# Separate accumulator banks, two pools for the second layer's banks, and a later split of its first weights

## The chip, the cores and the metric

The kernel runs on one core of a Trainium2 chip. The metric is the device time of one execution in microseconds, and the kernel before takes 818.07 us (median of three runs, 817.4 to 819.8). The core's engines run beside each other, each through its own queue in order: PE (matrix products), ACT (activations and copies), DVE (vector operations), POOL (GpSimd, vector operations too), and SP, which issues the transfers. An instruction waits in its queue until the instructions that produce its inputs, or that last used its buffer, are done.

## What is computed

The reference, cut to what matters:

```python
def _attn_ref(q, k, v, proj):                    # q, k, v: (2, 8, 768, 64), proj: (64, 6)
    q_bits = (np.einsum('bhsd,dk->bhsk', q, proj) > 0)
    k_bits = (np.einsum('bhsd,dk->bhsk', k, proj) > 0)
    mask = bucket(q_bits)[:, :, :, None] == bucket(k_bits)[:, :, None, :]
    scores = np.where(mask, scale * np.matmul(q, k.transpose(0, 1, 3, 2)), -1e9)
    attn = softmax(scores)
    return np.matmul(attn, v)

def _moe_ref(x, w_in, w_out):                    # x: (1536, 512), d_ff 2048
    h = np.maximum(x @ w_in, 0.0)
    return h * h @ w_out

def _moe2_ref(x, w_in, w_out, alpha):            # the same sizes
    h = x @ w_in
    g = np.maximum(h, 0.0) + alpha * np.minimum(h, 0.0)
    return g @ w_out

def reference(...):
    x = _attn_ref(q, k, v, proj) laid out as (1536, 512)
    return _moe2_ref(_moe_ref(x, ...), ...)
```

## The kernel before

The 1536 tokens go in four chunks of 384. Attention of chunk 0 runs alone; then `feed_forward(0)`, `(1)` and `(2)` compute the first layer of one chunk each, and between their steps the attention of the next chunk and the conversion of the weights are issued. `feed_forward(3)` follows with its output transposed (`project_t`), and then the second layer runs in two halves of 768 tokens: `wide_hidden(0)`, `whole_project(0)`, `wide_hidden(1)`, `whole_project(1)`. Every product is made of three matmuls, of operands that are split into a high and a low part: the high part is a rounding copy on ACT, the low part a subtraction on DVE or POOL.

In the first layer a step is one f of 16 (128 columns of d_ff). `hidden(c, f)` makes 12 matmuls (L704 to L706) into a bank, ACT takes the relu `r` out of it (L711) and makes `gh` (L712) and `g` (L714), and a subtraction makes `gl` (L717; on DVE in chunk 3). `project` adds the step before to the accumulators: one PSUM tile `acc` of three banks. After f = 15 of chunks 0 to 2 the banks are copied out in turn by DVE, ACT and DVE (L811, L813), and go to memory as `y`. In chunk 3 `project_t` uses these three banks and a fourth from the pool `ps_s` (L727, L728, and L730 or L735 with `gl`), which DVE and ACT copy out at L802 and L804. The weights of a step are split by ACT (L665, `wh`) and DVE or POOL (L666, `wl`).

In the second layer `wide_hidden(n)` makes, for each f of 8, seven products of 6 matmuls each (L896 to L898), from seven sums of x (`xph`, `xpl`: ACT L855, DVE L856; the plain sums L870, L875, L879 and L883 are DVE's). They are made by `x_sums(n)`. The weights of such an f come as one tile `wraw` (L911), which `w_part` splits: two copies on ACT (L918, 128x1024 and 128x768) and two subtractions on POOL (L919). Sums and the leaky relu (L902, L935, L942, L958) take the products out of the banks. `whole_project(n)` has 16 steps into six accumulator banks (L1000, L1001, L1006; in the last step L1003), which are then copied out by DVE (L1012) and ACT (L1014). Beside `whole_project(0)` go `second_x(2)`, which transposes chunk 2's y back (three blocks of four transposes, L838, each into one bank, copied by ACT at L839), `x_sums(1)`, and at its end the first `w_load` and `w_part` for `wide_hidden(1)`.

Before the change every bank of the second layer comes from one pool `ps2` with eight buffers of one tag, and a request gets a buffer that was given back. The order on each engine is set when the kernel is built, by a scheduler that follows the program, its priorities and its waits for buffers; on the chip each queue keeps that order.

Of the kernel before, what the change touches and what calls it, by code (L numbers as in the profile page):

```python
# [7 lines left out]
F32 = mybir.dt.float32  # L8
# [4 lines left out]
AF = mybir.ActivationFunctionType  # L13
ALU = mybir.AluOpType
PSUM = bass.MemoryType.PSUM
# [14 lines left out]
def kernel(  # L30
# [20 lines left out]
    nc = tc.nc  # L51
# [3 lines left out]
    P = 128  # L55
    T = S // 2
    NTB = T // P
    NKB = S // P
    NPAIR = H // 2
    NCH = NT // T  # L60
    KDM = DM // P
    KFF = w_in1.shape[0]
# [4 lines left out]
    def pool(name, bufs, stack=ctx, **kw):  # L67
        return stack.enter_context(tc.tile_pool(name=name, bufs=bufs, **kw))
# [1 line left out]
    const = pool("const", 1)  # L70
    dram = pool("scr", 1, space=DRAM)
    layer1 = ctx.enter_context(ExitStack())
    ps_s = pool("ps_s", 1, layer1, space=PSUM)
    ps_a = pool("ps_a", 1, layer1, space=PSUM)
    ps_h = pool("ps_h", 1, layer1, space=PSUM)
    ps_m = pool("ps_m", 2, layer1, space=PSUM)
    m1 = pool("m1", 1, layer1, side="right")
    m2 = pool("m2", 2, layer1, side="right")
    state_whole = pool("whole", 4, layer1, side="right")
# [2 lines left out]
    state = {"attention": True, "moe": False, "s": 0, "m": 0, "h": 0, "whole": state_whole}  # L82
# [28 lines left out]
    def h_tile():  # L111

        state["h"] += 1
        if not state["attention"] and state["h"] % 3:
            return ps_m.tile([P, 512], F32, tag="m", name="m")
        return ps_h.tile([P, 512], F32, tag="h", name="h")

    def f32(ap):
        return ap.bitcast(F32)
# [480 lines left out]
    def load_bits(u):  # L600
        l, f, o = u
        t = state["wide"].tile([P, DM, 2], U32, tag="wide", name="wbits")
        nc.sync.dma_start(out=t.rearrange("p n b -> p (n b)"), in_=(WO if o else WI)[l][f].bitcast(U32))
        w_bits[u] = t
# [67 lines left out]
    def units(i):  # L672

        if i >= len(work):
            return []
        return [(0, work[i][1], o) for o in range(2)]

    def fetch(i):

        for u in units(i):  # L680
            w_f[u] = state_whole.tile([P, DM], F32, tag="wf", name="wf")
            if u in w_d:
                nc.sync.dma_start(out=w_f[u], in_=w_d[u])
            else:
                to_f32(u, w_f[u])
                w_d[u] = dram.tile([P, DM], F32, tag="w%d_%d_%d" % u, name="w%d_%d_%d" % u)
                nc.sync.dma_start(out=w_d[u], in_=w_f[u])

    def split(i, o):
        for u in units(i)[o:o + 1]:  # L690
            last = i >= (NCH - 1) * KFF
            split_w(u, nc.gpsimd if (o or i // KFF == 1) and not last else nc.vector)

    def hidden(c, f, x, step):
        xh, xl = x
        wih, wil = w_split.pop((0, f, 0))
        ps = h_tile()
        hp = ps[:, 0:T]
        for kk in range(KDM):
            if kk == KDM // 2:  # L700
                step()
            ks = slice(kk * P, (kk + 1) * P)
            first, last = kk == 0, kk == KDM - 1
            nc.tensor.matmul(hp, wih[:, ks], xh[:, kk, :], start=first, stop=False)  # L704
            nc.tensor.matmul(hp, wih[:, ks], xl[:, kk, :], start=False, stop=False)  # L705
            nc.tensor.matmul(hp, wil[:, ks], xh[:, kk, :], start=False, stop=last)  # L706
        r = m1.tile([P, T], F32, tag="r", name="r")
        g = m1.tile([P, T], F32, tag="g", name="g")
        gh = m2.tile([P, T], F32R, tag="gh", name="gh")
        gl = m2.tile([P, T], F32R, tag="gl", name="gl")  # L710
        nc.scalar.activation(r, hp, AF.Relu)  # L711
        nc.scalar.activation(gh, r, AF.Square)  # L712
        if SQUARE[c] == "a":
            nc.scalar.activation(g, r, AF.Square)  # L714
        else:
            eng[SQUARE[c]].tensor_tensor(g, r, r, ALU.mult)
        (nc.vector if c == NCH - 1 else nc.gpsimd).tensor_tensor(gl, g, f32(gh), ALU.subtract)  # L717
        return gh, gl
# [19 lines left out]
    def project(f, g, acc, step):  # L738
        gh, gl = g
        woh, wol = w_split.pop((0, f, 1))  # L740
        first, last = f == 0, f == KFF - 1
        blocks = [slice(t * P, (t + 1) * P) for t in range(NTB)]

        def high(t):
            nc.tensor.matmul(acc[:, t, :], gh[:, blocks[t]], woh, start=first, stop=False)
            nc.tensor.matmul(acc[:, t, :], gh[:, blocks[t]], wol, start=False, stop=False)

        def low(t):
            nc.tensor.matmul(acc[:, t, :], gl[:, blocks[t]], woh, start=False, stop=last)  # L749

        if last:
            for t in range(NTB):
                high(t)
                low(t)
                step()
        else:
            for t in range(NTB):
                high(t)
                if t < NTB - 1:
                    step()  # L760
            for t in range(NTB):
                low(t)
            step()

    def feed_forward(c, background):

        slots = KFF * 5
        state["slot"] = 0

        turn = c == NCH - 1  # L770

        def step():
            state["slot"] += 1
            background(state["slot"] / slots)

        x = xT.pop(c)
        pend = None
        acc = None
        for f in range(KFF):
            i = index[c, f]  # L780
            split(i + 1, 0)
            split(i, 1)
            g = hidden(c, f, x, step)
            fetch(i + 2)
            for u in units(i + 3):
                if u not in w_d:
                    load_bits(u)
            step()
            if pend is not None:
                if acc is None:  # L790
                    acc = ps_a.tile([P, 3, 512], F32, tag="acc", name="acc")
                    if turn:
                        fourth = ps_s.tile([P, 2, 512], F32, tag="s", name="s")
                        acc = [acc[:, m, 0:T] for m in range(KDM - 1)] + [fourth[:, 0, 0:T]]
                (project_t if turn else project)(*pend, acc, step)
            pend = (f, g)
        (project_t if turn else project)(*pend, acc, step)
        if turn:
            x = new_raw(c)
            for m in range(KDM):  # L800
                if m % 2:
                    nc.vector.tensor_copy(x[:, m, :], acc[m])  # L802
                else:
                    nc.scalar.activation(x[:, m, :], acc[m], AF.Copy)  # L804
            return
        y = m1.tile([P, NTB, DM], F32, tag="y", name="y")
        d = dram.tile([P, NTB, DM], F32, tag=f"y{c}", name=f"y{c}")
        y_d[c] = d
        for t in range(NTB):
            if t % 2 == 0:  # L810
                nc.vector.tensor_copy(y[:, t, :], acc[:, t, :])  # L811
            else:
                nc.scalar.activation(y[:, t, :], acc[:, t, :], AF.Copy)  # L813
        nc.sync.dma_start(out=d, in_=y)


# [4 lines left out]
    def new_raw(c):  # L821
        x_raw[c] = state["xraw"].tile([P, KDM, T], F32, tag="xraw", name="xraw")
        return x_raw[c]
# [64 lines left out]
    def slot(name, dt=F32R):  # L888
        return state["slots"].tile([P, 2048], dt, tag="slot", name=name)

    def bank():
        return state["ps"].tile([P, 512], F32, tag="b", name="b")

    def products(ps, w, m, gh, gl, first, last):
        ms = slice(m * P, (m + 1) * P)
# [9 lines left out]
    raw_sums = {}  # L905
    loaded = {}

    def w_load(f):
        if f < NF:
            raw_sums[f] = slot("wraw", F32)[:, 0:7 * HM].rearrange("p (a n) -> p a n", n=HM)  # L910
            nc.sync.dma_start(out=raw_sums[f], in_=w_sum[f])  # L911

    def w_part(f):
        if f < NF:
            w = raw_sums.pop(f)
            t = [slot("wp")[:, 0:7 * HM].rearrange("p (a n) -> p a n", n=HM) for _ in range(2)]
            for i, j in ((0, 4), (4, 7)):
                nc.scalar.activation(t[0][:, i:j], w[:, i:j], AF.Copy)  # L918
                nc.gpsimd.tensor_tensor(t[1][:, i:j], w[:, i:j], f32(t[0][:, i:j]), ALU.subtract)  # L919
            loaded[f] = t  # L920

# [104 lines left out]
    for i in range(2):  # L1026
        low_ins, sm_ins = scored[0, 2, 2 * NTB - 1] if i == 0 else scored[0, 3, NTB - 1]
        with tc.issue_after(low_ins.ins), tc.issue_after(sm_ins.ins):
            fetch(i)
            if i == 0:  # L1030
                split(0, 0)
    state["moe"] = True


    steps, ends = attention_beside()
# [15 lines left out]
    for c in range(NCH - 1):  # L1051
        feed_forward(c, lambda x: beside(c + x))
# [17 lines left out]
        reason="needed late only",  # L1070
# [4 lines left out]
    feed_forward(NCH - 1, turned)  # L1075
    w_load(0)
    w_load(1)
    w_part(0)
    layer1.close()
    state["ps"] = pool("ps2", 8, space=PSUM)  # L1080
    state["g"] = pool("g", 1, side="right")
    state["sums"] = pool("sums", 2, side="right")
    state["out"] = pool("out", 2, side="right")

    steps = second_x(2, bank) + x_sums(1)

    def beside_project(f):
# [76 lines left out]
```

## Time and profile before

| | us |
|---|---|
| median of three runs | 818.07 |
| the three runs | 819.8, 818.07, 817.4 |
| the profiled execution | 819.41 |
| its span, first to last instruction | 817.4 |
| PE busy in the span | 776.8 |
| DVE busy | 545.8 |
| ACT busy | 505.8 |
| POOL busy | 313.3 |

The profiled execution has 2.0 us around its span. By stage, chunk 3 of the first layer lies from 490 to 560 us of the span, `wide_hidden(0)` from 560 to 622, `whole_project(0)` to 683 or so, `wide_hidden(1)` to 750, and the last projection behind it. A row of a timeline gives the start, the duration, the engine, the line and operation with its output and inputs, how many instructions the row holds, and, in brackets, how long the engine had been idle and what ended that.

### The profile page before, as it was taken

To read this page: it belongs to the slowest core of one execution; us is meant where nothing else is said; L and a number is where in the kernel's file an instruction comes from. 1 tells how busy PE (TensorE), PEld (TensorE's weight loads), DVE (VectorE), ACT (ScalarE), POOL (GpSimd) and SP (SyncE) were. 2 spreads that over 40 slices of the span, in tenths; PEclk is the share of its full clock that TensorE was granted. 3 is DMA by queue.
4 is the path that set the end of the run, shared out by engine and by line. 5 is a ranking of instruction groups with operands and counts; after the bars stand their busy time and mean duration, and the time that the engine had idled before them with its cause. 6 is when DMAs were issued, how large, how long until landed. Compare 5 with 4: busy or idle time off the path is not lost.

```text
span 817.4 us, 12516 instructions
## 1 busy us (share of the span) xinstructions
PE 776.8 (95%) x4330; PEld 634.9 (78%) x4330; DVE 545.8 (67%) x876; ACT 505.8 (62%) x988; POOL 313.3 (38%) x231
## 2 busy tenths in 40 slices
PE   6999899999999999999999998999999999999998
PEld 3665777776768767677776878999998888999886
DVE  8678899887757667788977956754665732665111
ACT  5778778766656556565665648764765525776331
POOL 1012323232356645643342355001563446663440
PEclk9999999999999999999999999999999999999999
DMA  6857878778678787677677568530311226421222
GB/s 181 212 159 229 259 228 269 241 218 243 174 223 265 225 226 242 210 242 264 203 237 232 174 218 286 171 130 1 135 27 52 65 95 221 141 68 44 65 65 90
DMA packets 56707, 143.66 MB, mean 176 GB/s; under 512 B 7402, under 2 KB 11652, under 8 KB 56644
## 3 DMA queue, kind: packets, MB, share of 16 engines
q1 hardware_dynamic: 56644, 142.87, 55.6%
q8 instruction: 34, 0.56, 0.3%
q14 instruction: 29, 0.24, 0.1%
HBM read 96.62 MB, written 25.47 MB: 149 GB/s over the span
## 4 chain that ended last, share of the span: by engine, by line
PE 44%; DVE 4%; DMA 3%; ACT 3%; issue 2%; POOL 1%; SPq 0%; ACTq 0%; POOLq 0%; DVEq 0%
PE b L1000 5%; PE b L1001 5%; PE b L1006 5%; PE b L896 4%; PE b L898 4%; PE b L897 4%; PE m L425 2%; PE h L704 1%; PE s L386 1%; PE h L705 1%; PE h L706 1%; PE acc L749 1%; PE m L409 1%; PE acc L728 1%; PE acc L735 1%
## 5 line engine op out<-in xcount | busy, mean ns | idle before, releaser
L666 POOL TENSOR_TENSOR wl<-wf,wh 128x512 fp32r<-128x512 f32 x64 | 89.0, 1393 | 82.1 <-ACT wh L665 76.4
L665 ACT ACTIVATE wh<-wf 128x512 fp32r<-128x512 f32 x128 | 79.5, 628 | 49.4 <-PE h L705 24.0
L919 POOL TENSOR_TENSOR wp<-wraw,wp 128x1024 fp32r<-128x1024 f32 (+1 forms) x32 | 68.4, 2161 | 99.8 <-ACT wp L918 92.1
L394 ACT ACTIVATE sm<-s,low 128x768 f32<-128x768 f32 x84 | 75.6, 901 | 45.9 <-DVE low L391 45.6
L717 POOL TENSOR_TENSOR gl<-g,gh 128x384 fp32r<-128x384 f32 x48 | 53.1, 1106 | 131.4 <-ACT g L714 64.9
L391 DVE TENSOR_REDUCE low<-s 128x1 f32<-128x768 f32 x84 | 80.0, 953 | 32.9 <-PE s L386 32.4
L990 POOL TENSOR_TENSOR gp<-g,gp 128x768 fp32r<-128x768 f32 x32 | 60.6, 1894 | 81.6 <-ACT gp L989 81.4
L386 PE MATMUL s<-k,q 128*128 128x384 f32 x336 | 80.0, 357 | 10.8 <-ACT sm L394 9.7
L409 PE MATMUL m<-ident,sm 128*128 128x128 f32 x531 | 85.4, 277 | 4.9 <-DVE pt L415 2.4
L409 PEld LDWEIGHTS m<-ident,sm 128*128 128x128 f32 x531 | 65.4, 141 | 22.7 <-DVE pt L415 3.4
L704 PE MATMUL h<-xh,wh 128*128 128x384 f32 x212 | 77.9, 367 | 2.1 <-DVE u L472 1.7
L386 PEld LDWEIGHTS s<-k,q 128*128 128x128 f32 x336 | 58.1, 192 | 26.9 <-ACT sm L394 16.8
L896 PE MATMUL b<-xph,wp 128*128 128x384 f32 x224 | 75.3, 343 | 3.4 <-DVE b L942 1.9
L1000 PE MATMUL b<-wp,gp 128*128 128x512 f32 x192 | 75.1, 391 | 0.0
L898 PE MATMUL b<-xph,wp 128*128 128x384 f32 x224 | 75.0, 335 | 0.0
L897 PE MATMUL b<-xpl,wp 128*128 128x384 f32 x224 | 75.0, 335 | 0.0
L1001 PE MATMUL b<-wp,gp 128*128 128x512 f32 x192 | 74.8, 389 | 0.0
L706 PE MATMUL h<-xh,wl 128*128 128x384 f32 x212 | 72.3, 341 | 0.3 <-POOL wl L666 0.3
L705 PE MATMUL h<-xl,wh 128*128 128x384 f32 x212 | 72.3, 341 | 0.0
L986 DVE TENSOR_TENSOR wp<-wp 128x512 fp32r<-128x512 f32 x28 | 23.1, 830 | 67.6 <-ACT wp L985 67.5
L425 PE MATMUL m<-pt,vr 128*64 128x384 f32 x336 | 66.2, 498 | 0.6 <-ACT pt L413 0.6
L666 DVE TENSOR_TENSOR wl<-wf,wh 128x512 fp32r<-128x512 f32 x64 | 50.9, 804 | 21.3 <-ACT wh L665 20.8
(180 smaller groups left out, 1829.8 us busy)
## 6 DMA issues: line engine op xcount, KB each, us to landing
wf<-w SPq DMA_DIRECT2D x96, 256.0 KB, 3.2
wbits<-in_w_in_dram SPq DMA_DIRECT2D x32, 512.0 KB, 4.6
wbits<-in_w_out_dram SPq DMA_DIRECT2D x32, 512.0 KB, 4.2
wraw<-ws SPq DMA_DIRECT2D x16, 896.0 KB, 4.7
q<-q SPq DMA_DIRECT2D x48, 192.0 KB, 3.2
w<-wf SPq DMA_DIRECT2D x32, 256.0 KB, 2.2
wp<-w SPq DMA_DIRECT2D x32, 256.0 KB, 2.5
k<-kh SPq DMA_DIRECT2D x14, 384.0 KB, 5.5
```

What stands on the lines that cost most here:

```text
L386: nc.tensor.matmul(ps[:, a, 0:HALF], self.q[:, h, i, qs], self.k[:, h, i, ks], start=i == 0, stop=i == 1)
L409: nc.tensor.transpose(ps[:, i * P:(i + 1) * P], pp[:, b * P:(b + 1) * P], ident)
L425: nc.tensor.matmul(self.o[r, 0:T], self.vr[:, b, r], self.pt[h][:, :, b, :], start=(b == 0), stop=(b == NKB - 1),)
L666: engine.tensor_tensor(lo, w, f32(hi), ALU.subtract)
L704: nc.tensor.matmul(hp, wih[:, ks], xh[:, kk, :], start=first, stop=False)
L705: nc.tensor.matmul(hp, wih[:, ks], xl[:, kk, :], start=False, stop=False)
L706: nc.tensor.matmul(hp, wil[:, ks], xh[:, kk, :], start=False, stop=last)
L896: nc.tensor.matmul(ps, w[0][:, ms], gh, start=first, stop=False, skip_group_check=True)
L897: nc.tensor.matmul(ps, w[0][:, ms], gl, start=False, stop=False, skip_group_check=True)
L898: nc.tensor.matmul(ps, w[1][:, ms], gh, start=False, stop=last, skip_group_check=True)
L1000: nc.tensor.matmul(a, g[:, 0, b], w[:, 0], start=f == 0, stop=False)
L1001: nc.tensor.matmul(a, g[:, 0, b], w[:, 1], start=False, stop=False)
```

## The change

It has three parts. The accumulator of the first layer becomes three tiles of one bank each (`acc0` to `acc2`), in a pool that is opened when chunk 0's attention is over. The second layer's banks get eight tags, and a running number of the request, modulo 8, sets the bank: banks 0 to 2 lie in the pool `ps_low` (on the place of `ps_h` and `ps_m`), banks 3 to 7 in `ps_high` (on that of `ps_s` and the accumulators). And the ACT copies of `w_part(0)`, before `wide_hidden(0)`, are ordered behind the relu of chunk 3's f = 12 (`KFF - 4`).

```diff
-    ps_s = pool("ps_s", 1, layer1, space=PSUM)
-    ps_a = pool("ps_a", 1, layer1, space=PSUM)
-    ps_h = pool("ps_h", 1, layer1, space=PSUM)
-    ps_m = pool("ps_m", 2, layer1, space=PSUM)
+    banks = ctx.enter_context(ExitStack())
+    ps_s = pool("ps_s", 1, banks, space=PSUM)
+    wide_banks = ctx.enter_context(ExitStack())
+    ps_a = pool("ps_a", 1, wide_banks, space=PSUM)
+    ps_h = pool("ps_h", 1, layer1, space=PSUM, side="right")
+    ps_m = pool("ps_m", 2, layer1, space=PSUM, side="right")
...
-        nc.scalar.activation(r, hp, AF.Relu)
+        state["relu", c, f] = nc.scalar.activation(r, hp, AF.Relu)
...
-                    acc = ps_a.tile([P, 3, 512], F32, tag="acc", name="acc")
+                    acc = [state["acc"].tile([P, 512], F32, tag=f"acc{t}", name=f"acc{t}") for t in range(NTB)]
                     if turn:
                         fourth = ps_s.tile([P, 2, 512], F32, tag="s", name="s")
-                        acc = [acc[:, m, 0:T] for m in range(KDM - 1)] + [fourth[:, 0, 0:T]]
+                        acc = [a[:, 0:T] for a in acc] + [fourth[:, 0, 0:T]]
...
-                nc.vector.tensor_copy(y[:, t, :], acc[:, t, :])
+                nc.vector.tensor_copy(y[:, t, :], acc[t])
             else:
-                nc.scalar.activation(y[:, t, :], acc[:, t, :], AF.Copy)
+                nc.scalar.activation(y[:, t, :], acc[t], AF.Copy)
...
     def bank():
-        return state["ps"].tile([P, 512], F32, tag="b", name="b")
+
+        i = state["bank"] % 8
+        state["bank"] += 1
+        return state["low" if i < 3 else "high"].tile([P, 512], F32, tag=f"b{i}", name="b")
...
+    def behind(later, earlier):
+
+        tc.add_manual_dep(
+            later.ins, earlier.ins.name,
+            mybir.DependencyInfo(mybir.DependencyClass.NoSync, mybir.DependencyReason.DATA),
+            reason="the order on their engine",
+        )
...
-                nc.scalar.activation(t[0][:, i:j], w[:, i:j], AF.Copy)
+                ins = nc.scalar.activation(t[0][:, i:j], w[:, i:j], AF.Copy)
+                if earlier is not None:
+                    behind(ins, earlier)
...
     state["moe"] = True
+    wide_banks.close()
+    state["acc"] = pool("ps_acc", 1, banks, space=PSUM)
...
-    w_part(0)
+    w_part(0, state["relu", NCH - 1, KFF - 4])
     layer1.close()
-    state["ps"] = pool("ps2", 8, space=PSUM)
+    state["bank"] = 0
+    state["low"] = pool("ps_low", 1, space=PSUM, side="right")
+    banks.close()
+    state["high"] = pool("ps_high", 1, space=PSUM)
```

In the changed kernel the lines move down: by 2 up to L883, then by 5 (L896 becomes L901), and by 12 to 15 from L918 on (L918 becomes L931, L919 L934, L1000 L1015, L1003 L1018, L1012 L1027).

Three places show how the order of instructions moves. The first is ACT's queue where chunk 2 ends and chunk 3 begins; `y<-acc` is the copy of the second accumulator bank, `wp<-wraw` the second layer's first split. Before:

```order
L665 ACTIVATE wh_5825<-wf 128x512
L918 ACTIVATE wp<-wraw 128x1024
L665 ACTIVATE wh_5875<-wf 128x512
L918 ACTIVATE wp<-wraw 128x768
L813 ACTIVATE y<-acc 128x512
L711 ACTIVATE r<-m 128x384
```

The same place in the changed kernel:

```order
L667 ACTIVATE wh_5835<-wf 128x512
L667 ACTIVATE wh_5887<-wf 128x512
L815 ACTIVATE y<-acc_4556 128x512
L713 ACTIVATE r<-m 128x384
L714 ACTIVATE gh<-r 128x384
```

The two copies of `wraw` have left this place.

The second is ACT's queue in the last steps of chunk 3, from the relu of f = 12 on. Before, it holds nothing but the steps' own work:

```order
L711 ACTIVATE r<-m 128x384
L712 ACTIVATE gh<-r 128x384
L714 ACTIVATE g<-r 128x384
L665 ACTIVATE wh_6474<-wf 128x512
L665 ACTIVATE wh_6430<-wf 128x512
L711 ACTIVATE r<-m 128x384
```

In the changed kernel, from the row right behind that relu on:

```order
L667 ACTIVATE wh_6486<-wf 128x512
L714 ACTIVATE gh<-r 128x384
L716 ACTIVATE g<-r 128x384
L931 ACTIVATE wp<-wraw 128x1024
L667 ACTIVATE wh_6442<-wf 128x512
L931 ACTIVATE wp<-wraw 128x768
L931 ACTIVATE wp<-wraw 128x1024
L713 ACTIVATE r<-m 128x384
L931 ACTIVATE wp<-wraw 128x768
L714 ACTIVATE gh<-r 128x384
L716 ACTIVATE g<-r 128x384
L667 ACTIVATE wh_6490<-wf 128x512
```

Two pairs of copies stand in these rows, and a third pair follows in the next step; each pair is followed by its two subtractions on POOL, which has no other instructions between the six. Before, the first pair stood at the end of chunk 2, the second early in chunk 3, the third in `wide_hidden(0)`.

The third is PE's queue in `whole_project(0)`: `b<-ident,yb` are the four transposes of the third block of `second_x(2)`. Before, they stand behind a middle step:

```order
L1006 MATMUL b<-wp,gp 128x512 x6
L838 MATMUL b<-ident,yb 128x128 x4
L1000 MATMUL b<-wp,gp 128x512
```

In the changed kernel they stand in the last step, behind the first two accumulator banks' last matmuls:

```order
L1018 MATMUL b<-wp,gp 128x512
L1015 MATMUL b<-wp,gp 128x512
L840 MATMUL b<-ident,yb 128x128 x4
L1016 MATMUL b<-wp,gp 128x512
```

The block is the 41st request for a bank and has the number of the first accumulator bank of `whole_project(0)`, so these transposes wait for DVE's copy of that bank. The work of `x_sums(1)` that needs the block follows on DVE behind the first two of these copies:

```order
L1027 COPY y<-b 128x512 x2
L872 TENSOR_TENSOR xt<-xraw 128x768
L858 TENSOR_TENSOR xpl<-xraw,xph 128x768 x2
L858 TENSOR_TENSOR xpl<-xt,xph 128x768
L877 TENSOR_TENSOR xt<-xraw,xt 128x768
L881 TENSOR_TENSOR xraw<-xraw 128x768
L885 TENSOR_TENSOR xraw<-xraw,xt 128x768
L858 TENSOR_TENSOR xpl<-xt,xph 128x768
L858 TENSOR_TENSOR xpl<-xraw,xph 128x768 x2
L1027 COPY y<-b 128x512
L907 TENSOR_TENSOR u_7746<-b,p_7738 128x384
```

Before, all ten of these sums and differences stood in front of the last seven weight splits of `whole_project(0)`, and `wide_hidden(1)` followed its copies directly.

## Rows read from the trace of the kernel before

**Rows 1.** The page: busy time of PE, share of the span, instructions.

```profile
PE 776.8 (95%) x4330; PEld 634.9 (78%) x4330; DVE 545.8 (67%) x876; ACT 505.8 (62%) x988; POOL 313.3 (38%) x231
```

**Rows 2.** Windows: stretch, its length, then busy time by engine; one stage.

```profile
622.00:683.00 61.00, 61.00 (x276) 50.51 (x275) 27.52 (x25) 26.89 (x40) 28.08 (x15) 1.00 0.25 85
```

**Rows 3.** Waits of PE, whole span: waited for, us in total, times, longest.

```profile
PE acc L727 <- ACT gh L712: 1.8, 1, 1.8
...
PE b L896 <- ACT xraw L804: 1.2, 1, 1.2
...
PE m L838 <- DMA yb<-y: 0.5, 1, 0.5
```

**Rows 4.** Timeline, end of chunk 2 and start of chunk 3.

```profile
488.25 0.34 PE L706 MATMUL m<-xh,wl 128*128 128x384 f32 x1
...
490.07 0.68 DVE L811 COPY y<-acc 128x512 f32<-128x512 f32 x1
...
490.78 0.60 ACT L813 ACTIVATE y<-acc 128x512 f32<-128x512 f32 x1 [2.43 <-DVE y L811]
...
492.43 0.44 PE L727 MATMUL acc<-gh,wh 128*128 128x384 f32 x1 [1.76 <-ACT gh L712]
```

**Rows 5.** Timeline, start of the second layer.

```profile
559.16 0.49 ACT L804 ACTIVATE xraw<-acc 128x384 f32<-128x384 f32 x1 [0.62 <-DVE xraw L802]
...
559.71 0.44 PE L896 MATMUL b<-xph,wp 128*128 128x384 f32 x1 [1.17 <-ACT xraw L804]
```

**Rows 6.** Timeline, last steps of chunk 3.

```profile
541.94 0.49 ACT L711 ACTIVATE r<-m 128x384 f32<-128x384 f32 x1 [1.38 <-PE m L706]
...
542.47 0.53 ACT L712 ACTIVATE gh<-r 128x384 fp32r<-128x384 f32 x1
...
542.90 0.51 ACT L714 ACTIVATE g<-r 128x384 f32<-128x384 f32 x1
...
543.57 1.16 ACT L665 ACTIVATE wh<-wf 128x512 fp32r<-128x512 f32 x2 [0.16 <-DMA wf<-w]
...
552.95 0.69 DVE L666 TENSOR_TENSOR wl<-wf,wh 128x512 fp32r<-128x512 f32 x1 [0.63 <-ACT wh L665]
...
555.92 0.56 DVE L717 TENSOR_TENSOR gl<-g,gh 128x384 fp32r<-128x384 f32 x1 [2.28 <-ACT g L714]
...
556.60 0.38 PE L730 MATMUL acc<-gl,wh 128*128 128x384 f32 x1
```

**Rows 7.** Timeline, DVE and POOL beside each other, and each alone.

```profile
506.44 4.66 POOL L919 TENSOR_TENSOR wp<-wraw,wp 128x1024 fp32r<-128x1024 f32 x2 [2.31 <-issue]
...
506.87 2.53 DVE L666 TENSOR_TENSOR wl<-wf,wh 128x512 fp32r<-128x512 f32 x1 [0.78 <-ACT wh L665]
...
509.32 2.60 DVE L856 TENSOR_TENSOR xpl<-xraw,xph 128x768 fp32r<-128x768 f32 x1
...
528.91 0.95 DVE L856 TENSOR_TENSOR xpl<-xt,xph 128x768 fp32r<-128x768 f32 x1
...
568.93 4.22 POOL L919 TENSOR_TENSOR wp<-wraw,wp 128x1024 fp32r<-128x1024 f32 x2 [57.83 <-ACT wp L918]
...
691.30 4.21 POOL L919 TENSOR_TENSOR wp<-wraw,wp 128x1024 fp32r<-128x1024 f32 x2 [2.83 <-PE b L898]
...
692.75 0.62 DVE L935 SCALAR_TENSOR_TENSOR g<-b,neg_alpha,up 128x384 f32<-128x384 f32 x1 [1.97 <-ACT b L934]
```

**Rows 8.** Timeline, `whole_project(0)` and the start of `wide_hidden(1)`.

```profile
637.43 0.60 PE L838 MATMUL b<-ident,yb 128*128 128x128 f32 x4
...
680.11 8.36 POOL L919 TENSOR_TENSOR wp<-wraw,wp 128x1024 fp32r<-128x1024 f32 x4 [2.50 <-issue]
...
683.25 0.39 PE L1003 MATMUL b<-wp,gp 128*128 128x512 f32 x1
...
690.16 1.79 ACT L918 ACTIVATE wp<-wraw 128x1024 fp32r<-128x1024 f32 x2 [1.53 <-DMA wraw<-ws]
...
696.43 0.33 PE L896 MATMUL b<-xph,wp 128*128 128x384 f32 x1
```

More of the change, by code (lines that the diff above doesn't have):

```diff
@@ L744, in high @@
         def high(t):
-            nc.tensor.matmul(acc[:, t, :], gh[:, blocks[t]], woh, start=first, stop=False)
-            nc.tensor.matmul(acc[:, t, :], gh[:, blocks[t]], wol, start=False, stop=False)
+            nc.tensor.matmul(acc[t], gh[:, blocks[t]], woh, start=first, stop=False)
+            nc.tensor.matmul(acc[t], gh[:, blocks[t]], wol, start=False, stop=False)
         def low(t):
-            nc.tensor.matmul(acc[:, t, :], gl[:, blocks[t]], woh, start=False, stop=last)
+            nc.tensor.matmul(acc[t], gl[:, blocks[t]], woh, start=False, stop=last)
         if last:
@@ L911, in w_load, with w_part @@
             nc.sync.dma_start(out=raw_sums[f], in_=w_sum[f])
-    def w_part(f):
+    def w_part(f, earlier=None):
         if f < NF:
```

## The prediction

> **What bounds the kernel now.** I read the busy times first: PE has work in 776.8 of the span's 817.4 us [rows 1], and in whole_project(0) in all of its 61.00 us [rows 2]. So PE's queue is the bound, and an edit is worth what it takes from or adds to PE's idle time. Then the waits of PE: three places belong to what the change touches, 1.8 us at L727, 1.2 us at L896 and 0.5 us at L838 [rows 3]. Then the timeline around these and around every place where the order moves. The profiled execution took 819.41 us, 1.34 above the median of the runs; I sum against it and carry the difference over to the median. A measurement of this kernel can tell about 0.3% (2.45 us) from no change.
>
> **Part 1, three accumulator tiles.** At the end of chunk 2 the three copies of y go one behind the other, although they read different banks: ACT's copy at 490.78 was released by DVE's at 490.07 [rows 4]. The relu of chunk 3's first step stands behind it on ACT, and the hidden product that it reads had been done since the matmul of 488.25. PE then waits 1.76 us for gh [rows 4]. With a tile for each bank, ACT's copy waits for PE alone, and the two copies of wraw that stood ahead of it have left; the relu can start when the product is done, before the next hidden product is through. That wait goes: **-1.8**. The y of chunk 2 then goes to memory earlier, and the 0.5 us at L838, where its way back is waited for [rows 3], should go too: **-0.5**. At the ends of chunks 0 and 1 no wait of this kind is among the rows for PE, so nothing is gained there: I count it as nothing, hidden by the attention's matmuls.
>
> **Part 2, two pools.** The first matmul of the second layer waits 1.17 us for ACT's copy of the last accumulator [rows 5], although it reads nothing from it: the new pool wanted the old banks back. In the changed kernel the first bank lies on the place of ps_h and ps_m, whose last reader was done long before: **-1.2**. The first bank of ps_high is asked for 24 matmuls later and is free by then.
>
> The fixed rotation has a price elsewhere. The third block of second_x(2) gets the number of the first accumulator of whole_project(0), so its four transposes move from 637.43 [rows 8] to the last step, behind DVE's copy of that bank, and most of x_sums(1) with them. PE reaches the place 0.60 us earlier, having left the transposes out. The first bank is done at 683.25 + 0.39 - 0.60 = 683.04; a copy by DVE of 0.68 [rows 4], the transposes of 0.60 and a copy by ACT of 0.60 [rows 4] follow, with some 0.3 for three handovers: 685.2. Then DVE has ten sums and differences, each 0.95 alone [rows 7], so 9.5, and behind them in its queue the fifth bank's copy, two sums and a leaky relu, 0.6 each [rows 7], 2.4 together: 697.1. PE's order has 51 matmuls of wide_hidden(1) ahead of the one that needs the last of these; before, PE was through with 51 at 696.43 [rows 8]. Without disturbance the step costs 697.1 - 696.4 = **+0.7**.
>
> It will be disturbed. Where DVE has an operation with two inputs in SBUF and POOL a subtraction of weights, each waits for the whole of the other and they take turns: beside POOL's pair of 4.66 us at 506.44, DVE's split took 2.53 and its x part 2.60, against 0.69 and 0.95 alone [rows 6, 7]; an operation that reads a bank isn't slowed (0.62 at 692.75, while POOL was at 691.30 to 695.5 [rows 7]). Before, x_sums lay clear of the weights' subtractions. Now it meets them: the second pair of the four that took 680.11 to 688.47 [rows 8], and the next pair, whose copies on ACT start at 690.16 when their weights land [rows 8]. Taking turns, DVE waits for the rest of one subtraction (0.85, since the second pair starts at about 683.7 and its first subtraction takes 2.36 of the 4.22 by its share of the columns), and for three whole ones (1.86, 2.36, 1.86): 6.9 us. The end moves to 704.0, which is **+7.6**. The ends are +0.7 and +7.6; I take the upper, since the rows with both engines at work lie there.
>
> **Part 3, the later split.** ACT's six copies, and behind them POOL's six subtractions, all fall into the last three steps of chunk 3. The first copy stands behind relu, weight copy, gh and g of that step: 541.94 + 0.49 + 0.58 + 0.53 + 0.51 + 1.04 = 545.1 [rows 6] (1.04 is the larger one's share of 1.79 [rows 8]). ACT has the room: its steps leave 1.5 of each 4.16 us, and gh and g come in time for PE by my count. DVE has not. In these steps it has six operations with both inputs in SBUF, three weight splits of 0.69 and three gl of 0.56 [rows 6], and the last projection needs the last two. POOL has 3 x 4.22 = 12.66 us of subtractions [rows 7]. In turns, all are through at 545.1 + 12.66 + 3 x 0.69 + 3 x 0.56 = 561.5; before, the last gl was ready at 555.92 + 0.56 = 556.48, and PE took it at 556.60 [rows 6]. That is **+4.9**. If the last gl had only to wait for POOL's last end, without the other five in between, it would be 545.1 + 12.66 + 0.56 = 558.3, or +1.7; if DVE were served first each time, about 0. I take +4.9 for the same rows' sake, and keep 0 for the range. The pair of 568.93 that goes from wide_hidden(0) to the tail [rows 7] gives nothing back, since PE doesn't wait for POOL there.
>
> **The sum.** -1.8 - 0.5 - 1.2 + 4.9 + 7.6 = +9.0. On the profiled execution 819.4 + 9.0 = 828.4; on the median 818.07 + 9.0 = 827.1, so **827**, slower by 1.1%.
>
> **A rule that speaks for the change.** At 490.07 and 490.78 two engines read different banks one behind the other, and PE pays 1.76 us for it [rows 4]. The Trainium skill, Perfetto Trace Analysis, section on optimizing tensor performance, says that independent groups of matmuls should rotate through different banks, so that taking one out lies beside the next group's matmuls. By that rule alone the change is worth its three waits, -3.5, and the time would be 814.6. The trace bears the rule out for the accumulators; the same rotation, made rigid, is what hands the third block an occupied bank in the second layer.
>
> **Rivals.**
> - The change as it is meant: DVE is served first. If DVE's next operation always goes ahead of POOL's next subtraction, x_sums runs through at +0.7 and gl is late by 0 to 1: -3.5 + 0.7 + 0 = -2.8, 815.3, **faster**. It decides at the sum of both collisions: under 1.05 us it is faster by more than 0.3%. Against it stand the 2.53 and 2.60 of DVE's two operations in turn [rows 7]: the second should then not have waited for a subtraction that began after the first. I give 0.05.
> - The tail is absorbed. POOL may start so early, or the weights' splits lie so far ahead of PE, that the last gl is late by 0 to 1.7, while x_sums goes as reckoned: 818.07 - 3.5 + 7.6 + (0 to 1.7) = 822.2 to 823.9. For it: in each step gl is ready well ahead of the matmul that needs it, save in the last. Chance 0.16.
> - x_sums is hidden: the next weights land late enough that POOL is idle while DVE works, or PE's order has more to do meanwhile. 818.07 - 3.5 + 4.9 + (0.7 to 2) = 820.2 to 821.5. Chance 0.10, half of it within 0.3%.
> - It goes worse: DVE's delay is handed on to the next f, because the fifth and sixth bank are copied out behind x_sums and outputs and the next weights queue behind them on SP; or the 1.8 us of the boundary stay because ACT's copy waits for a late load of weights. Another 3 to 8 us, 830 to 835. Chance 0.14.
> - The change does not do what it says: with the boundary's wait kept and the rest as reckoned it is 828.9, inside the forecast's own range; I count it there.
>
> **How the numbers follow.** The forecast, both collisions near their upper ends, has 0.55 and its own range is 824 to 830. The range reaches down to the middle of the third rival and up over half of the fourth: **820.5 to 832**, which leaves out the first rival, half of the third and about half of the fourth, under 2 in 10. Faster by over 0.3% means under 815.6: 0.05. Within 0.3% (815.6 to 820.5): half of the third rival and a little of the first and second, 0.08. Slower: 0.87.
>
> **What would show it.** Part 1: no wait of PE at the first L729 of chunk 3, and ACT's y copy before DVE's second one. Part 2: the second layer's first matmul right behind the last projection; the last L840 behind L1027's first copy, DVE's sums behind it with durations of 2.3 to 2.9 beside POOL, and waits of PE in the first 10 us of wide_hidden(1) that add up to 7 or 8 us. Part 3: six subtractions on POOL between 543 and 561, and PE waiting for gl before the last L732 matmuls for 4 to 5 us. The prediction is wrong if DVE's operations beside POOL stay at 0.6 to 1.0, or if PE's idle time in these two places is under 3 us together.

## The result

The changed kernel takes 826.78 us (median of six runs, 825.04 to 828.69), the one before beside it 818.14 (six runs). That is slower, by 8.6 us between the medians. The measured ratio of the two is 1.0087, 95% interval 1.0068 to 1.0107, which is 7.1 us (5.6 to 8.8). The forecast was 9.0. The profiled execution of the changed kernel took 825.86 us with a span of 824.1; against the profiled execution of before (819.41) that is 6.5 us. It is 2.2 less than the medians differ by, since the profiled execution of before lies 1.3 above its median and that of the changed kernel 0.9 below its own.

The page of the changed kernel, first row of the busy times, and the window that answers to [rows 2]:

```profile
PE 778.9 (95%) x4330; PEld 636.4 (77%) x4330; DVE 545.9 (66%) x876; ACT 505.9 (61%) x988; POOL 315.5 (38%) x231
```

```profile
622.00:683.00 61.00, 61.00 (x274) 50.50 (x273) 11.74 (x16) 22.91 (x33) 26.61 (x15) 1.00 0.28 87
```

PE has 2.1 us more of busy time for the same 4330 matmuls, and in whole_project(0) DVE has 11.7 us of work where it had 27.5 [rows 2]: most of x_sums(1) has left. The waits of PE over the whole span, those that touch the change; the columns are those of [rows 3]:

```profile
PE b L902 <- DVE xpl L858: 2.7, 2, 2.3
PE b L901 <- ACT xph L857: 1.7, 2, 0.9
...
PE acc L732 <- DVE gl L719: 1.6, 1, 1.6
...
PE acc L730 <- DVE wl L668: 1.2, 1, 1.2
PE m L840 <- DMA yb<-y: 1.1, 1, 1.1
```

The 1.8 us at the start of chunk 3 and the 1.2 us at the start of the second layer [rows 3] are gone. In their place PE waits 2.8 us for the last wl and gl of chunk 3, and 4.4 us for x_sums at the start of wide_hidden(1).

The start of chunk 3 in the timeline, against [rows 4]:

```profile
485.36 0.69 DVE L813 COPY y<-acc 128x512 f32<-128x512 f32 x1
...
486.32 0.58 ACT L815 ACTIVATE y<-acc 128x512 f32<-128x512 f32 x1
...
487.06 0.69 DVE L813 COPY y<-acc 128x512 f32<-128x512 f32 x1
...
490.75 0.33 PE L729 MATMUL acc<-gh,wh 128*128 128x384 f32 x1
```

The three copies end at 487.75 and not at 492.10, and the first matmul into chunk 3's accumulators has no wait in its bracket. The tail of chunk 3, POOL and DVE:

```profile
543.75 14.46 POOL L934 TENSOR_TENSOR wp<-wraw,wp 128x1024 fp32r<-128x1024 f32 x6 [58.98 <-ACT wp L931]
...
544.23 2.47 DVE L668 TENSOR_TENSOR wl<-wf,wh 128x512 fp32r<-128x512 f32 x1 [0.91 <-ACT wh L667]
547.85 0.98 DVE L719 TENSOR_TENSOR gl<-g,gh 128x384 fp32r<-128x384 f32 x1 [1.15 <-ACT g L716]
548.75 2.89 DVE L668 TENSOR_TENSOR wl<-wf,wh 128x512 fp32r<-128x512 f32 x1
551.56 2.19 DVE L719 TENSOR_TENSOR gl<-g,gh 128x384 fp32r<-128x384 f32 x1
553.68 2.87 DVE L668 TENSOR_TENSOR wl<-wf,wh 128x512 fp32r<-128x512 f32 x1
556.47 2.16 DVE L719 TENSOR_TENSOR gl<-g,gh 128x384 fp32r<-128x384 f32 x1
...
558.68 0.44 PE L732 MATMUL acc<-gl,wh 128*128 128x384 f32 x1 [1.64 <-DVE gl L719]
```

Six subtractions on POOL in a row, and six operations on DVE between them; five of the six take over 2 us where they take 0.69 and 0.56 alone [rows 6]. The start of wide_hidden(1):

```profile
684.68 0.66 PE L840 MATMUL b<-ident,yb 128*128 128x128 f32 x4
...
686.44 1.30 DVE L872 TENSOR_TENSOR xt<-xraw 128x768 f32<-128x768 f32 x1
687.66 3.44 DVE L858 TENSOR_TENSOR xpl<-xraw,xph 128x768 fp32r<-128x768 f32 x2
691.02 0.95 DVE L858 TENSOR_TENSOR xpl<-xt,xph 128x768 fp32r<-128x768 f32 x1
691.89 3.13 DVE L877 TENSOR_TENSOR xt<-xraw,xt 128x768 f32<-128x768 f32 x1
694.94 2.58 DVE L881 TENSOR_TENSOR xraw<-xraw 128x768 f32<-128x768 f32 x1
...
680.36 9.05 POOL L934 TENSOR_TENSOR wp<-wraw,wp 128x1024 fp32r<-128x1024 f32 x4 [2.51 <-issue]
691.52 5.18 POOL L934 TENSOR_TENSOR wp<-wraw,wp 128x1024 fp32r<-128x1024 f32 x2 [2.11 <-ACT wp L931]
...
690.28 0.69 PE L902 MATMUL b<-xpl,wp 128*128 128x384 f32 x1 [2.27 <-DVE xpl L858]
```

The transposes stand behind the first copy of y, DVE's sums behind them, and POOL's subtractions stretch four of the ten. In the kernel before, the same ten stood beside POOL's subtractions of another tile (`gp`) and three of them were stretched too, but PE was at work all the while [rows 2]. The timeline of before, POOL and DVE in the middle of whole_project(0):

```profile
638.60 1.85 POOL L990 TENSOR_TENSOR gp<-g,gp 128x768 fp32r<-128x768 f32 x1 [2.68 <-ACT gp L989]
...
639.04 2.22 DVE L870 TENSOR_TENSOR xt<-xraw 128x768 f32<-128x768 f32 x1 [2.17 <-ACT xraw L839]
...
643.53 2.60 DVE L856 TENSOR_TENSOR xpl<-xt,xph 128x768 fp32r<-128x768 f32 x1
```

### The profile page after: what moved, and what is told of

The parts are those of the page before. It is cut to its first block, busy times and chain, and to the rows that moved or that the text cites. A ratio compares the mean times of both kernels' runs of the same rounds, so it can differ in the third digit from the quotient of the medians.

```text
span 824.1 us, 12519 instructions
## 1 busy us (share of the span) xinstructions
PE 778.9 (95%) x4330; PEld 636.4 (77%) x4330; DVE 545.9 (66%) x876; ACT 505.9 (61%) x988; POOL 315.5 (38%) x231
## 4 chain that ended last, share of the span: by engine, by line
PE 44%; DVE 7%; issue 2%; DMA 2%; ACT 1%; POOL 1%; SPq 0%; DVEq 0%; POOLq 0%; ACTq 0%
PE b L1015 5%; PE b L1016 5%; PE b L1021 5%; PE b L901 4%; PE b L902 4%; PE b L903 4%; PE m L427 2%; PE h L706 1%; PE h L707 1%; PE s L388 1%; PE acc L751 1%; PE h L708 1%; DVE wl L668 1%; PE acc L747 1%; PE m L411 1%
## 5 line engine op out<-in xcount | busy, mean ns | idle before, releaser
L934 POOL TENSOR_TENSOR wp<-wraw,wp 128x1024 fp32r<-128x1024 f32 (+1 forms) x32 | 70.7, 2234 | 104.3 <-ACT wp L931 100.3
L901 PE MATMUL b<-xph,wp 128*128 128x384 f32 x224 | 75.6, 345 | 3.3 <-ACT xph L857 1.7
L1001 DVE TENSOR_TENSOR wp<-wp 128x512 fp32r<-128x512 f32 x28 | 20.5, 732 | 85.7 <-ACT wp L1000 85.7
L1015 PE MATMUL b<-wp,gp 128*128 128x512 f32 x192 | 75.0, 390 | 0.0
```

What stands on the lines that cost most here:

```text
L901: nc.tensor.matmul(ps, w[0][:, ms], gh, start=first, stop=False, skip_group_check=True)
L1015: nc.tensor.matmul(a, g[:, 0, b], w[:, 0], start=f == 0, stop=False)
```

## The experiments

All were timed in five rounds beside the kernel before. A table by stage tells the causes apart better than the totals: the order of instructions up to chunk 3 is the same in most of these kernels, but their profiled executions reach the last matmul of chunk 2 anywhere from 482.6 to 493.0 us, so totals of single executions say little. The four columns are worked out, in us, from the timelines of one execution each, from start to start: from the last matmul into chunk 2's accumulators to the first into chunk 3's; from there to the first matmul of the second layer; from there to the first copy of y of whole_project(0); from there to the end of the span.

| kernel | ratio to before, 95% interval | start of chunk 3 | chunk 3 | to first y | to the end |
|---|---|---|---|---|---|
| before | | 6.36 | 67.28 | 123.97 | 133.72 |
| changed | 1.0087 (1.0068 to 1.0107) | 4.42 | 69.79 | 123.39 | 140.17 |
| e1, other bank | 1.0038 (1.0018 to 1.0058) | 4.40 | 70.92 | 124.54 | 134.07 |
| e2, early split | 1.0046 (1.0024 to 1.0068) | 4.44 | 66.23 | 123.37 | 140.46 |
| e3, x free | 1.0108 (1.0082 to 1.0135) | 4.43 | 71.48 | 123.97 | 140.40 |
| e4, tail free | 1.0068 (1.0044 to 1.0091) | 4.42 | 68.22 | 123.36 | 140.96 |
| tiles alone | 0.9987 (0.9968 to 1.0007) | 4.42 | 67.25 | 123.95 | 133.90 |
| late split alone | 1.0055 (1.0029 to 1.0081) | 4.44 | 71.22 | 123.95 | 134.23 |
| e1 and e2 together | 0.9973 (0.9958 to 0.9987) | 4.44 | 66.59 | 123.86 | 134.17 |
| spread split | 0.9978 (0.9957 to 1.0000) | 4.43 | 66.39 | 123.86 | 133.90 |
| e5, x held | 1.0042 (1.0019 to 1.0064) | 4.39 | 72.57 | 123.50 | 134.60 |
| e6, tail held | 1.0073 (1.0049 to 1.0098) | 4.40 | 66.73 | 124.58 | 140.34 |
| e7, f = 8 | 1.0054 (1.0034 to 1.0073) | 4.43 | 73.96 | 123.92 | 134.25 |

**The occupied bank (e1_other_bank).**

```diff
...
-    steps = second_x(2, bank) + x_sums(1)
+    spares = iter((6, 7, 6))
+    steps = second_x(2, lambda: bank(next(spares))) + x_sums(1)
...
+    state["bank"] = 40
...
```

The rotation goes on with bank 0 in wide_hidden(1), one earlier than in the changed kernel.

> The changed kernel, but the third block of second_x(2) takes bank 6 again, not the first accumulator's, so that it stands in the middle of whole_project(0) as before. Theory (the occupied bank costs 0.7 to 7.6 us, about 6 by the trace after): about 820.5, 1.003 of before. Rival (the cost comes from the rigid rotation within wide_hidden(1) or from the outputs and weights on SP): no better than 825.

Measured 822.25 us, 1.0038; the last column falls from 140.17 to 134.07, where before has 133.72. The third block's place is all but 0.4 us of the loss behind the first projection; the fixed rotation within wide_hidden costs nothing that shows. The total is 1.7 us above what was expected (the ratio 0.0008), and the chunk 3 column is 1.1 longer than in the changed kernel's execution, with the same order there.

**The early split (e2_early_split).**

```diff
-    w_part(0, state["relu", NCH - 1, KFF - 4])
+    w_part(0)
```

> The changed kernel without the order behind f = 12: the first splits of the second layer's weights stand at the end of chunk 2 and early in chunk 3 again. Theory (six subtractions in the tail cost 3 to 5 us): about 823.3, 1.006 of before. Rival (the tail's delay only takes the place of the wait at the start of chunk 3, which comes back with the copies of wraw): about 826, 1.009.

Measured 823.19 us, 1.0046. Chunk 3 falls to 66.23 us, and the start of chunk 3 stays at 4.44, although the two copies of wraw stand at the end of chunk 2 again. So the later split is what makes the tail longer, and with separate tiles the gain at the start of chunk 3 doesn't need it.

**Each part alone.** The tiles alone are the kernel before with acc0 to acc2; the late split alone is the kernel before with the order behind the relu of f = 12.

> The kernel before with the three accumulator tiles alone: one pool of eight banks for the second layer, first splits early. Theory (the serial copies of one tile cost 1.8 us): the time from the last accumulator matmul of chunk 2 to the first of chunk 3 falls from 6.4 to 4.4 us, the 1.2 us at the second layer's start stay, about 816.3, 0.998 of before. Rival (the wait at the start of chunk 3 is ACT's copies of wraw): no change, 818.1.

> The kernel before with the later split alone. Theory (the tail pays for POOL's six subtractions): from the relu of f = 12 to the second layer's first matmul 20 to 22 us where before has 17.8, about 821.5, 1.004 of before, and the wait at the start of chunk 3 stays, since the copies of the one tile stay in turn. Rival (moving wraw's copies away from the end of chunk 2 pays for it): 818.1.

The tiles alone took 818.78 us, 0.9987, no difference from before that the interval shows, though the stage shows the 1.9 us (4.42 for 6.36); the late split alone took 823.66, 1.0055, with 71.22 us for chunk 3. From the relu of f = 12 to the second layer's first matmul it takes 21.9 us, within what was expected. Its start of chunk 3 is 4.44 too, against my expectation: with one tile, but without wraw's copies and subtractions, the wait goes as well. The row that I had passed over stands ahead of DVE's first copy in the trace of before:

```profile
487.18 4.64 POOL L919 TENSOR_TENSOR wp<-wraw,wp 128x1024 fp32r<-128x1024 f32 x2 [2.67 <-ACT wp L918]
...
487.65 2.49 DVE L666 TENSOR_TENSOR wl<-wf,wh 128x512 fp32r<-128x512 f32 x1 [0.78 <-ACT wh L665]
```

By these rows the wait needed both: POOL's subtractions held DVE up until 490.07, and the one tile handed that on to ACT. Either part of the change takes it away. With one tile, no run moves POOL's subtractions without ACT's copies of wraw; that it is POOL is read from DVE's 2.49 us, where a split takes 0.69 alone [rows 6].

**Both undone (e1e2_both_undone), and the splits apart (spread_split).** The first is e1 and e2 in one. The second is e1 with the three pairs behind the relu of f = 2, the relu of f = 10, and the first p of wide_hidden(0):

```diff
...
-            w_part(f + 1)
+            w_part(f + 1, {(0, 0): state["relu", NCH - 1, 10], (0, 1): state.get("p1")}.get((n, f)))
...
-    w_part(0, state["relu", NCH - 1, KFF - 4])
+    w_part(0, state["relu", NCH - 1, 2])
...
```

> The changed kernel with the third block in bank 6 and the first splits early again: what is left is the accumulator tiles and the two pools. Theory (both collisions are the whole loss): the three waits go and nothing comes, about 815, 0.996 of before. Rival (the fixed rotation costs on its own in wide_hidden): 818 or more.

> The changed kernel with the third block in bank 6, and the three first splits apart from each other: behind the relu of f = 2, behind that of f = 10, and behind the first p of wide_hidden(0). Theory (a pair of subtractions is hidden where the next steps have slack, and costs only in a row or in the last step): about 815, 0.996 of before. Rival (every pair beside chunk 3 costs about 1 us): 817.

816.77 us (0.9973, interval below 1) and 816.67 us (0.9978, interval up to 1.0000): both beat the changed kernel by some 9 us, and the first is faster than the kernel before. Both are some 1.7 us above their theories, and the second's total is nearer to its rival's 817; it is the stage that speaks against the rival, since chunk 3 takes 66.39 us with two pairs spread in it and 66.59 with the splits early. The tiles and the two pools are worth about 2 us, less than the 3.5 that their waits add up to.

**What makes the late x_sums dear (e3_x_free, e5_x_held).** e3 leaves out POOL's subtractions for f = 1 and 2 of wide_hidden(1). e5 holds ACT's copies for f = 3 behind x_sums as well:

```diff
...
+            if state["part"] == 11:
+                earlier = state["x_part", 1, 2]
...
-                nc.gpsimd.tensor_tensor(t[1][:, i:j], w[:, i:j], f32(t[0][:, i:j]), ALU.subtract)
-            loaded[f] = t
+                if keep:
+                    nc.gpsimd.tensor_tensor(t[1][:, i:j], w[:, i:j], f32(t[0][:, i:j]), ALU.subtract)
+            loaded[f] = t if keep else [t[0], t[0]]
...
```

> The changed kernel with POOL's subtractions left out for f = 1 and 2 of wide_hidden(1): the high part stands in for the low part there, so part of the computation is changed. x_sums(1) stays behind the occupied bank. Theory (taking turns with POOL is most of the price): DVE's ten operations take 9.5 us together, PE's waits in the first 20 us of wide_hidden(1) fall from 5 to under 2 us, about 821.5, 1.004 of before. Rival (the late start of x_sums alone is the price): about 826.

> As e3_x_free (POOL's subtractions for f = 1 and 2 of wide_hidden(1) left out, the high part in place of the low part), but ACT's copies for f = 3 are ordered behind the last copy of x_sums(1), so that ACT no longer waits there for the weights of f = 3 ahead of x_sums. Theory (DVE and POOL in turns are the larger part of the price of the occupied bank): DVE's ten operations run without a gap in 9 to 10 us, and from the first copy of y to the end 135 to 137 us, where the changed kernel has 140.2 and the one before 133.7; about 823, 1.005 of before. Rival (the late start is the price, with or without POOL): 139 to 141 us.

e3 came out against my theory: 828.9 us, 1.0108, and 140.40 us to the end. PE waits 3.4 us at the start of wide_hidden(1), not under 2. Its trace shows why it can't tell the two causes apart: the slots that came free moved the copies for f = 3 up on ACT, ahead of the last copies of x_sums, where the first of them waited 1.42 us for its weights; POOL's subtraction then met DVE's next part (2.55 us).

```profile
697.38 1.06 ACT L935 ACTIVATE wp<-wraw 128x1024 fp32r<-128x1024 f32 x1 [1.42 <-DMA wraw<-ws]
...
699.20 2.55 DVE L858 TENSOR_TENSOR xpl<-xt,xph 128x768 fp32r<-128x768 f32 x1 [1.43 <-ACT xph L857]
```

e5 keeps the order of the changed kernel up to the last copy of x_sums, and DVE's sums run through. The timeline of e5, DVE, from the first sum to the last part, and POOL beside it:

```profile
690.72 0.95 DVE L872 TENSOR_TENSOR xt<-xraw 128x768 f32<-128x768 f32 x1
691.58 1.82 DVE L858 TENSOR_TENSOR xpl<-xraw,xph 128x768 fp32r<-128x768 f32 x2
...
694.19 0.95 DVE L877 TENSOR_TENSOR xt<-xraw,xt 128x768 f32<-128x768 f32 x1
...
697.66 1.82 DVE L858 TENSOR_TENSOR xpl<-xraw,xph 128x768 fp32r<-128x768 f32 x2
...
684.64 4.20 POOL L941 TENSOR_TENSOR wp<-wraw,wp 128x1024 fp32r<-128x1024 f32 x2 [2.51 <-issue]
699.85 4.21 POOL L941 TENSOR_TENSOR wp<-wraw,wp 128x1024 fp32r<-128x1024 f32 x2 [11.02 <-ACT wp L937]
```

Ten operations in 8.8 us, against 14.6 in the changed kernel (686.44 to 700.99), and 134.60 us to the end. With x_sums as late as in the changed kernel, but POOL out of its way, 0.9 us of the 6.45 is left, and PE waits 0.5 us and not 4.4. So the late start alone costs next to nothing. Nor do the turns alone: in the kernel before, three of the ten operations took 2.2 to 2.6 us beside POOL, early enough that PE didn't wait. The price comes of both together, turns with POOL at a place where PE needs the sums at once. By the Trainium skill, SBUF — State Buffer, section "SBUF: two separate sides", DVE and GpSimd have a pair of ports in common that one of them holds for its whole instruction; the trace agrees (2.58 and 3.13 us beside a subtraction, 0.95 without).

**What holds up the tail (e4_tail_free, e6_tail_held).** The same for the first layer's tail: e4 leaves out the six subtractions, e6 also holds the copies for f = 3 behind the first p of wide_hidden(0).

> The changed kernel with POOL's six subtractions of the tail of chunk 3 left out (f = 0 to 2 of wide_hidden(0); the high part stands in for the low part, so part of the computation is changed); ACT's six copies stay. Theory (POOL and DVE in turns hold up the last wl and gl): PE's 1.2 and 1.6 us before the last projection go, and about 823.5, 1.006 of before. Rival (ACT's copies make gh and g late): no change, 826.5.

> As e4_tail_free (POOL's first six subtractions of the second layer left out, the high part in place of the low part), but the copies for f = 3 are ordered behind the first p of wide_hidden(0), so that no subtraction at all falls into the tail of chunk 3; ACT's six copies stay there. Theory (POOL alone holds the tail up): from the first matmul into the accumulators of chunk 3 to the first of the second layer 66.2 to 66.8 us, as with the early splits, where the changed kernel has 69.8; about 823, 1.006 of before. Rival (ACT's copies are part of it): 67.5 to 69.

e4 took 825.85 us, 1.0068, with 68.22 us in chunk 3, between the theory and its rival: a fourth pair had moved into the room that was left, and PE's 1.6 us for gl stayed.

```profile
553.75 4.62 POOL L939 TENSOR_TENSOR wp<-wraw,wp 128x1024 fp32r<-128x1024 f32 x2 [67.27 <-ACT wp L935]
...
554.22 2.48 DVE L668 TENSOR_TENSOR wl<-wf,wh 128x512 fp32r<-128x512 f32 x1 [0.91 <-ACT wh L667]
556.62 2.16 DVE L719 TENSOR_TENSOR gl<-g,gh 128x384 fp32r<-128x384 f32 x1
```

One pair in the last step costs some 2 us. In e6 no subtraction is left in the tail, ACT's six copies are, and chunk 3 takes 66.73 us, within 0.5 of the early split's 66.23; the last step's wl and gl are back to their own length:

```profile
556.63 0.69 DVE L668 TENSOR_TENSOR wl<-wf,wh 128x512 fp32r<-128x512 f32 x1
559.60 0.56 DVE L719 TENSOR_TENSOR gl<-g,gh 128x384 fp32r<-128x384 f32 x1 [2.27 <-ACT g L716]
```

So it is POOL, not ACT. e6's total of 1.0073 is higher than this stage gives (3 us less than the changed kernel would be 1.005), and its interval of plus or minus 2 us reaches to it only just. Of the difference, 1.2 us stand in the next column, 124.58 for 123.39: in wide_hidden(0) PE waits 1.0 us there for a copy p on ACT, which stands behind copies of weights that had waited 3.57 us for POOL.

**Four steps earlier (e7_f8).** e1 with `KFF - 8` in place of `KFF - 4`.

> The changed kernel with the third block in bank 6 and the order behind the relu of f = 8 in place of f = 12; the three pairs then stand between the relus of f = 8 and f = 12. Theory (six subtractions cost where the last projection stands right behind them, and are hidden where later steps give DVE time): from chunk 3's first accumulator matmul to the second layer's first 66.4 to 67 us, about 816.5, 0.998 of before. Rival (the work of DVE and POOL is too much wherever it stands in a row): 69 us and more, 819.5.

My theory fell: 823.84 us, 1.0054, with 73.96 us in chunk 3, more than with the order behind f = 12. The row of five subtractions runs to 543.6, and PE waits for gl in the steps beside it. The timeline of POOL:

```profile
530.25 13.31 POOL L935 TENSOR_TENSOR wp<-wraw,wp 128x768 fp32r<-128x768 f32 x5 [4.75 <-ACT wp L932]
```

Its waits of PE:

```profile
PE acc L737 <- DVE gl L719: 4.9, 3, 2.7
```

The row counts, and not only the last step. In the forecast's own terms six subtractions and the six operations of three steps are 12.66 + 3.75 = 16.4 us of work that excludes each other, an estimate, and three steps of 4.16 us have 12.5. One pair at a time is hidden in spread_split; in the last step, as e4 shows, even one pair costs 2 us.

## Why the prediction was right, and where its steps were off

**The bound.** PE's queue was the bound, and the time went where PE waits. That held, but for some 2 us that PE's own work took longer at a lower clock; they stood in no term of the forecast.

**Part 1.** Priced at -1.8, measured -1.9. The cause was told too narrowly: the one tile needed POOL's hold on DVE to cost anything, as the late split alone shows. The -0.5 at L840 failed: the wait grew from 0.5 to 1.1 us. The y of chunk 2 does leave earlier, but PE comes to its transposes earlier too, and the way through memory took 8.7 us to that matmul, where before took 6.3 (why it took longer is not shown):

```profile
487.82 0.32 SPq L816 DMA_DIRECT2D y<-y  x1
...
496.56 0.63 PE L840 MATMUL m<-ident,yb 128*128 128x128 f32 x4 [1.13 <-DMA yb<-y]
```

**Part 2, the start.** Priced at -1.2, and the wait is gone. The wait that I had called the new pool's went with the two pools; the tiles alone leave 0.7 us of it.

**Part 2, the bank.** Priced at +7.6, with +0.7 as the price of the late start without POOL. In the table it is 6.45 in the last column less 0.58 in the one before: +5.9. The late start alone is, in the same two columns of e5, 0.9 less 0.5: +0.4. The term was mis-sized by 1.7. DVE's ten operations lost 14.6 - 8.8 = 5.8 us and not 6.9: they met four subtractions, as forecast, but lost 0.35, 1.62, 2.18 and 1.63 us to them, where the forecast had 0.85, 1.86, 2.36 and 1.86. Alone, too, they take 8.8 us and not the 9.5 of the forecast. The path was off as well. The forecast let PE wait once, at the 52nd matmul of wide_hidden(1), for the end of DVE's queue, and named 7 or 8 us of waits as its sign. PE waited at earlier matmuls, 4.4 us in all and 2.27 at the second, for parts of x_sums, and reached the 52nd without a wait. The rest of the 5.9 is slower matmuls: up to the 52nd PE was busy for 11.5 us where before has 9.1, at the lower clock that the last section shows. That the two together came within 1.7 us of the one wait that was forecast is in part luck.

**Part 3.** Priced at +4.9. In the changed kernel's profiled execution the stage chunk 3 is 2.5 us longer, in which the second layer's start has gained 1.2 and L840 lost 0.6, so the tail cost some 3.1; PE's waits in it are 2.8, for wl and gl, where the forecast's sign was 4 to 5. The forecast added all twelve operations to 16.4 us; they took 14.9, from 543.75 to 558.63, since one gl ran almost freely (0.98 us) and the others took less than the sum gives them. In the three other executions with six late subtractions and the same order (e1, e3, e5) the stage is 70.9 to 72.6 us, 1.1 to 2.8 longer than there. With these the tail is 4 to 6 us, around the forecast. Those executions have a lowered clock in or behind the tail (below), the changed kernel's has not. By the ratios, which rest on many executions, the later split costs 3.4 us (changed against e2), 4.5 (alone) or 5.3 (e1 against both undone), each with an uncertainty of 2 us or so. How often the timed executions of the changed kernel fall to the lower clock in the tail isn't known. Their mean granted clock is 0.988 to 0.994, with 0.993 in the profiled one and the lowest in the longest; that fits more falls, but doesn't say where.

**The sum.** By the profile it is -1.9 + 2.5 - 0.6 + 6.45 = +6.5, by the ratio +7.1, by the medians +8.6; forecast +9.0. The two collisions were named with place and cause, and each is shown by a kernel that takes it away. That the total came so near owes something to luck: the gains were forecast at 3.5 and are some 2.2 (both undone), the losses at 12.5 and are some 9.3 (changed against both undone, by the ratios), and the two errors offset each other in part.

**The rivals.** That DVE is served first is refuted by the alternating rows. A tail absorbed by the steps is refuted by PE's 2.8 us in it, and by e7 even where steps follow. That x_sums is hidden is true only without POOL (e5). The rule of the Trainium skill on rotating banks (Perfetto Trace Analysis, section "Optimizing Tensor Performance") is borne out less than the prediction says: the three accumulators had a bank each before too, what changed is that they are three tiles, and the late split alone takes the same wait away with one tile. The tiles and the two pools together are worth about 2 us, as e1 and e2 in one show.

## What to carry to other kernels

Before a piece of work is moved, look at which engine's operations it will stand beside: here POOL's subtractions and DVE's operations with two inputs in SBUF excluded each other, and a move that only seemed to change a place cost 6 us, though the same operations had met other work of POOL at no cost where they stood before. A fixed rotation of buffers decides who waits for whom by counting; count the requests up to the first odd consumer. And when an experiment takes work away, compare the order of what is left, since e3 and e4 each gave their cause's place to something else.

## What the runs showed of the hardware that was not expected

The granted clock fell to its lower level (1.2 GHz, 0.50 in the rows, more where a window holds both levels) behind some of these waits. In the changed kernel PE had waited 2.27 us for x_sums when it did; windows of the changed kernel, PE's busy time as first figure behind the comma and the granted clock as third from the end:

```profile
688.00:690.00 2.00, 0.02 (x1) 0.00 (x0) 2.00 (x1) 1.10 (x2) 1.41 (x1) 1.00 0.93 341
690.00:692.00 2.00, 1.72 (x5) 1.72 (x6) 2.00 (x4) 1.06 (x1) 0.48 (x1) 0.57 0.96 222
...
694.00:696.00 2.00, 1.11 (x8) 0.79 (x6) 2.00 (x2) 0.84 (x1) 2.00 (x2) 1.00 0.84 329
```

A matmul there took 0.52 us and not 0.33, and some ten of them make up most of the 2.1 us more of PE's busy time. The clock fell at this place in all five traces in which x_sums came late beside POOL (the changed kernel, e2, e3, e4 and e6), and not in e5. In the tail of e1 PE was busy for 1.30 of the 4 us from 555 to 559, and the clock stood at 0.50 right after; in the changed kernel's own tail it was busy for 1.18 of the same 4 us, and the clock stayed at 1.00. Windows of e1:

```profile
555.00:557.00 2.00, 0.45 (x1) 0.19 (x1) 2.00 (x2) 0.00 (x0) 2.00 (x2) 1.00 0.00 0
557.00:559.00 2.00, 0.85 (x5) 0.85 (x6) 1.10 (x1) 0.36 (x1) 0.69 (x1) 0.99 0.26 36
559.00:561.00 2.00, 2.00 (x8) 2.00 (x7) 0.56 (x1) 0.62 (x2) 0.00 (x0) 0.50 0.84 333
```

Windows of the changed kernel:

```profile
555.00:557.00 2.00, 0.82 (x4) 0.28 (x2) 2.00 (x2) 0.00 (x0) 2.00 (x2) 1.00 0.00 0
557.00:559.00 2.00, 0.36 (x3) 0.32 (x3) 1.62 (x1) 0.00 (x0) 1.21 (x1) 1.00 0.00 0
559.00:561.00 2.00, 2.00 (x13) 2.00 (x12) 0.81 (x2) 0.98 (x2) 0.00 (x0) 1.00 0.75 244
```

The late split alone shows the fall behind the same two waits as the changed kernel's tail (1.20 and 1.64 us), and e3 and e5 show it too. So the same order of instructions in the tail gave a fall in three traces (e1, e3, e5) and none in the changed kernel's, and a wait of this length costs itself or itself and 1 to 2 us more. What decides between them stays open.
